# Interleaved multi-query and linear attention on one core: read-outs ahead of flips at a stage's entry, a pause ahead of a weight, and features closed at the second bankful

## The chip, the cores and the metric

The kernel runs on one core of a Trainium2 chip. The metric is the device time of one execution in microseconds (us); the time of the kernel before is the median of three runs. A profile is one further execution, recorded by the hardware. Engines are named as in the profile: PE is TensorE (PEld its weight loads), DVE is VectorE, ACT is ScalarE, POOL is GpSimd, SP is SyncE, whose queue issues nearly all DMAs. L623 is line 623 of the kernel.

## The reference

Four sub-layers are applied to `x` of shape [1, 2048, 576], in float32, each with a layer normalisation without parameters ahead of it and a residual around it:

```python
def _A_ref(x, wq, wk, wv, wo):                 # 32 query heads of 18, one key and value head
    scores = jnp.einsum("bhqd,bkd->bhqk", q, k) * (Dh ** -0.5)
    p = _softmax(scores, axis=-1)
    o = jnp.einsum("bhqk,bkd->bhqd", p, v)
    return ... @ wo

def _B_ref(x, wqkv, w_phi, wo):                # 32 heads of 18, linear attention
    pq = jnp.einsum("bhsd,hdf->bhsf", q, w_phi)
    pk = jnp.einsum("bhsd,hdf->bhsf", k, w_phi)
    phi_q = jnp.concatenate([_softmax(pq), _softmax(-pq)], axis=-1)
    phi_k = jnp.concatenate([_softmax(pk), _softmax(-pk)], axis=-1)
    kv = jnp.einsum("bhsf,bhsd->bhfd", phi_k, v)
    z  = jnp.einsum("bhsf->bhf", phi_k)
    num = jnp.einsum("bhqf,bhfd->bhqd", phi_q, kv)
    den = jnp.einsum("bhqf,bhf->bhq", phi_q, z)[..., None] + 1e-6
    return ... (num / den) @ wo

x = x + _A_ref(_layernorm(x), ...)
x = x + _B_ref(_layernorm(x), ...)
x = x + _A_ref(_layernorm(x), ...)
x = x + _B_ref(_layernorm(x), ...)
```

## The kernel before

Tokens are worked in 16 tiles of 128. The kernel's loop runs over two layers, each an A and a B sub-layer, in two stages.

**The attention stage** goes through score units. For each unit TensorE multiplies keys by queries (`score`, L518), ScalarE takes the exponential (L985), and TensorE multiplies by the values (`values`, L797), which accumulates in a bank of PSUM. Between the bursts of units a generator, `stream`, puts other work, one step a turn: in layer 0 the folding of the feature map into the linear layer's weights (`fold_phi`, L337 to L362), the output projections of finished tiles (`finish_tile`), and for tiles 0 to 12 the linear layer's own keys, values and queries (`mix`). A "bankful" is one half (288 columns) of a projection of one tile. The loads of weights are generators too, advanced once a turn: `load_weight` fetches a weight in five pieces through three staging buffers, and VectorE splits each piece into a high part (L133) and a low part (L134). The order of PE and DVE in this stage is pinned to the order in which the code emits it. One bank of PSUM is free for the other work besides the one that the accumulation leaves, so a matmul of the other work waits until the copy that empties a bank has run.

**Features.** `feature_start` takes a bankful, subtracts the maximum and the minimum of each head and applies the exponential (L551 to L558); `feature_end` sums each head's values and divides (reduce L563, reciprocal L564, multiply L565). With `copies` equal to `V`, as in `mix`, all but the exponential is VectorE's work; with `A`, in the stage's entry, the multiply of L565 is GpSimd's. `update_state` (L595, added at L601) adds a tile's product of features and values to `kv`. The normalised query features of a tile are "flipped" (transposed on TensorE, eleven transposes, L623, and copied by ScalarE, L628) and spilled to DRAM.

**The read-out stage** is entered by `leave()`: the last keys and values, `finish_state` (eight transposes of `kv`, L731, and three DMAs that write the block-diagonal `kvb`, L736), and the queries of three tiles which are left: tile 13 with its features in `featk`, tile 14 in `featq`, tile 15 in `xsc`. Within `leave` the order of PE is pinned. Their flips come behind it, from `flips`. Then `token_tile(i)` runs for all 16 tiles in a pipeline, up to the next stage: it loads the features `pht` (L645), and `read_out` makes 22 matmuls (44 in the profile's count, L748), the division on VectorE (`den`, `xo`, L755 to L758), five transposes (L290, L294), which ScalarE (L131) and VectorE (L134, L299) copy as a high and a low part into `xs`, and the output projection with `wob` (L240, two bankfuls), added to the residual. In layer 0 the next layer's norm and queries follow. Here the tile framework's scheduler orders what is not pinned, and seven banks of PSUM rotate.

Of the kernel before, what the change touches and what calls it, by code (L numbers as in the profile page):

```python
# [61 lines left out]
def kernel(ctx, tc, x_in, wq, wk, wv, wo, wqkv, w_phi, wob, out):  # L62
# [174 lines left out]
    def project(dst, w, c0, xs, after=None, products=range(len(PRODUCTS)), last=LASTP):  # L237
        for j, n in enumerate(products):
            slot, half, k = PRODUCTS[n]
            T.matmul(dst, xs[:, slot, :], w[half][:, k, c0 : c0 + HALF],  # L240
                     start=(n == 0), stop=(n == last))
            if n == last:
                if after is not None:
                    after()
                yield -250
            elif j % 2:
                yield 250
# [4 lines left out]
    def bankful(kind, ps, shape=(P, HALF)):  # L252
        yield Kind(kind)
        return ps.tile(list(shape), F32, name="ps")

    def run(gen):
        for _ in gen:
            pass
# [301 lines left out]
    def feature_end(e, b, E):  # L560
        ev = e[:, b * HH : (b + 1) * HH].rearrange("p h s d -> p (h s) d")
        z = small.tile([P, 2 * HH], F32, name="fz")
        V.tensor_reduce(z, ev, axis=AX.X, op=ALU.add)  # L563
        V.reciprocal(z, z)  # L564
        E.tensor_mul(ev, ev, z[:, :, None].to_broadcast([P, 2 * HH, DH]))  # L565

    def heads(po):
        return po.rearrange("p (h d) -> p h d", d=DH)
# [37 lines left out]
    def queries(xs, e, st, ps, copies):  # L606
        for b in range(2):
            po = yield from bankful("P", ps)
            yield from project(po, st["wpq"], b * HALF, xs, lambda: feature_start(heads(po), e, b, copies))
        if copies is A:  # L610
            for b in range(2):
                feature_end(e, b, G)
        else:
            feature_end(e, 0, V)

    def flip_features(e, pht, ps, copies):
        phi = e.rearrange("p h s d -> p (h s d)")
# [78 lines left out]

    def queries_in(i, xs, eq, st, ps, spill):
        yield from queries(xs, eq, st, ps, A)
        pht = st["sp"].tile([P, NKG, P], F32, name="phs", bufs=2)
        yield from flip_features(eq, pht, ps, A)  # L700
        spill_features(pht, spill, i)
# [169 lines left out]
    def attend(layer, st, a1o, stream):  # L871
# [13 lines left out]
        with ctx1:  # L885
# [11 lines left out]
            def finish_group(c, g):  # L897
                turned = a1.tile([P, CW], F32, name="turned", bufs=2)
                V.transpose(turned, acc[c, g])
                yield STAGE  # L900
                sums = turned.rearrange("p (b f) -> p b f", f=32)
                rd = small.tile([P, CW // 32], F32, name="rd")
                V.reciprocal(rd, sums[:, :, DH])
                V.tensor_mul(sums, sums, rd[:, :, None].to_broadcast([P, CW // 32, 32]))
                yield STAGE
                osb = a1.tile([P, CW], F32, name="osb", bufs=1)
                V.transpose(osb, turned)
                parts = a1.tile([P, 2, CW], F32R, name="parts", bufs=1)
                split(parts[:, 0, :], parts[:, 1, :], osb, V, V)
                keep_group(parts.bitcast(F32), c, g)  # L910
                if g == NG - 1:
                    while c > 0 and c - 1 not in st["added"]:
                        yield STAGE
                    on = heads_in()
                    load_heads(on.bitcast(F32), c)
                    due = at[0] + DUE
                    while at[0] < min(due, len(units)):
                        yield STAGE
                    finished.append((c, on))
                yield STAGE  # L920
# [294 lines left out]
    for layer in range(LAYERS):  # L1215
        last = layer == LAYERS - 1
        st.update(start_state(bw), added=set())
        with tc.tile_pool(name="a1o", bufs=2) as a1o:

            def load(key, place, *args, **kw):  # L1220
                st[key] = weight_tiles(place) if isinstance(place, str) else place.weights()
                yield from reload_weight(key) if key in wd else load_weight(st[key], *args, **kw)

            def load_wo():
                return load("wo", Room(a1o), wo, slice(0, D))

            def load_wv():
                return load("wv", "b", wqkv, slice(2 * D, 3 * D))

            def stream(v, layer=layer):  # L1230
# [34 lines left out]
                loads.append(load_wo())  # L1265
                if layer == 0:
                    yield from wait(lambda: len(loads) > 0)
                    loads.extend((save_weight("wo"), save_weight("wq"), load_wv(), load("wob", "a", wob, slice(0, D)),
                                  save_weight("wob")))

                    def room(name):
                        if name == "wt":
                            return bw.tile([P, 5 * P], F32, name="xn")
                        tag = {"fo": "featk", "bd": "featq"}[name]
                        return bw.tile([P, H, 2, DH], F32, name=tag).rearrange("p h s d -> p (h s d)")

                    for step in fold_phi(ps, room, v.a1):
                        yield step
                        if finished and not isinstance(step, Kind) and (step is STAGE or step < 0):
                            yield from finish_tile()  # L1280
                else:
                    loads.append(load_wv())
# [128 lines left out]
        with psx, tc.tile_pool(name=f"s{layer + 1}", bufs=2) as sp:  # L1411
            if not last:
                reload_w4(sp)

            def leave():
                xn = layer_norm(c, stats, sp, A, "xo")
                advance(second_keys)
                xl = sp.tile([P, 9, P], F32R, name="xs3")
                advance(transposed(xn, xl, ps, A, LOE), 2)
                queued = [queries_in(i, x, feature_room(name), st, ps, spills[layer])  # L1420
                          for i, x, name in ((KEPT, kept, "featk"), (c - 1, xs, "featq"))]
                advance(queued[0])
                both = sp.tile([P, 9, PW], F32R, name="xsc").bitcast(F32).rearrange("p a b -> p (a b)")
                ek, eq = (both[:, k * 2 * D : (k + 1) * 2 * D].rearrange("p (h s d) -> p h s d", s=2, d=DH)
                          for k in range(2))
                last_keys = keys_in(c, xl, ek, st, ps)
                queued.append(queries_in(c, xl, eq, st, ps, spills[layer]))
                advance(last_keys, 2)
                run(load("wob", "a", wob, slice(0, D), engines=(A, V)))
                advance(last_keys, 2)  # L1430
                if not last:
                    run(load("wq", "b", wq, slice(0, D), engines=(A, G)))
                advance(queued[0])
                advance(last_keys)
                advance(queued[2])
                run(finish_state(st, sp, ps))
                advance(queued[2])
                advance(queued[1], 2)
                before = None
                for i in traced(nc)[mark:]:  # L1440
                    if i.engine == mybir.EngineType.PE:
                        if before is not None:
                            tc.add_manual_dep(i, before, NOSYNC, reason="order")
                        before = i.name
                return queued

            def flips(queued):
                for job in queued:
                    run(job)
                    yield STAGE  # L1450

            def room(i):
                if i % 2:
                    return sp.tile([P, NKG, P], F32, name="pht", bufs=1)
                return bw.tile([P, NKG, P], F32, name="pht")

            def token_tile(i):
                pht = room(i)
                load_features(pht, spills[layer], i)
                if i not in left:  # L1460
                    xres[i] = sp.tile([P, D], F32, name="xt", bufs=6)
                    nc.sync.dma_start(xres[i], xd[i])
                yield STAGE
                yield STAGE
                yield from read_out(i, pht, st, sp, ps)
                if last:
                    nc.sync.dma_start(out[i * P : (i + 1) * P, :], xres[i])
                else:
                    nc.sync.dma_start(xd[i], xres[i])
                    yield STAGE  # L1470
                    yield from next_queries(i, None, layer + 1, st, bw, sp, ps)

            order = range(NT)
            st["sp"] = sp
            jobs = [flips(leave()), *[token_tile(i) for i in order]]
            if last:
                run(pipelined(jobs))
            else:
                settle(layer + 1, ps, jobs)

# [26 lines left out]
```

## Time and profile before

| what | us |
|---|---|
| median of three runs | 2711.44 (2710.91 to 2713.7) |
| the profiled execution | 2709.95 |
| its span in the trace | 2708.2 |
| TensorE busy in the span | 2616.8 (97%) |
| ScalarE busy | 2154.5 (80%) |
| VectorE busy | 1236.9 (46%) |

The mean granted clock of TensorE is 0.99 of full speed. The read-out stage of layer 0 begins about 1283 us into the span, that of layer 1 about 2598 us. A row of the timeline gives the start and the length of a group of equal instructions, the engine, the line, the operation, what it writes and reads, and in brackets the idle time of the engine just before it with what ended it. A row such as "PE ps L623 <- POOL featq L565: 8.3, 4, 2.7" in the table of waits says that TensorE's instructions of L623 waited for GpSimd's L565 four times, for 8.3 us together and 2.7 at the longest.

### The profile page before, as it was taken

The numbers are of one execution on the slowest core, as the hardware profiler recorded it, in microseconds if no ns is written. First come the engines' busy times: TensorE is split into PE (matmuls) and PEld (weight loads), VectorE is DVE, ScalarE is ACT, GpSimd is POOL, SyncE is SP. The second block draws the span as 40 slices with busy tenths as digits, with TensorE's granted clock in tenths as the row PEclk, the third lists the DMA queues.
The fourth block names the chain that finished last, engine by engine and source line by source line (L and its number), as shares of the span: only waits on it lengthen the run. The fifth ranks groups of instructions, "written<-read, shape, count | busy, mean of one in ns | idle before, by whom it ended". The sixth has DMA issues, their size and how long they took to land. (4 is left out here: it accounts for less than half of the span.)

```text
span 2708.2 us, 55518 instructions
## 1 busy us (share of the span) xinstructions
PE 2616.8 (97%) x22052; PEld 1447.8 (53%) x22052; DVE 1236.9 (46%) x2839; ACT 2154.5 (80%) x2529; POOL 65.9 (2%) x106
## 2 busy tenths in 40 slices
PE   7989899999999999999999999999999999999999
PEld 6633335554555544437997244444444444444588
DVE  8532244445455444435775124444444444444365
ACT  4578898898989889995334999999999999999721
POOL 1000000000000000001100000000000000000010
PEclk9999999999999999999999999999999999999999
DMA  5564134222223212224645412222222222222164
GB/s 185 160 205 134 52 105 133 72 65 55 59 63 74 62 45 56 58 64 131 197 151 167 146 50 59 59 59 59 59 59 59 59 59 59 56 58 56 39 192 139
DMA packets 469358, 245.06 MB, mean 90 GB/s; under 512 B 213410, under 2 KB 426850, under 8 KB 469090
## 3 DMA queue, kind: packets, MB, share of 16 engines
q1 hardware_dynamic: 467618, 238.46, 31.7%
q8 instruction: 177, 2.90, 0.5%
q10 hardware_dynamic: 1472, 2.95, 0.4%
q14 instruction: 91, 0.75, 0.1%
HBM read 133.86 MB, written 105.51 MB: 88 GB/s over the span
## 5 line engine op out<-in xcount | busy, mean ns | idle before, releaser
L985 ACT ACTIVATE pt<-sc 128x1024 f32<-128x1024 f32 x2036 | 1922.7, 1055 | 206.9 <-PE sc L518 187.2
L518 PE MATMUL sc<-qst,kst 56*128 56x512 f32 x3840 | 699.0, 452 | 26.4 <-ACT pt L985 26.0
L518 PEld LDWEIGHTS sc<-qst,kst 56*128 56x128 f32 x3840 | 320.2, 184 | 566.2 <-ACT pt L985 512.9
L797 PE MATMUL acc<-pt,vst 128*32 128x512 f32 x4096 | 502.6, 602 | 1.5 <-DVE kv L601 0.9
L797 PE MATMUL ps<-pt,vst 128*32 128x512 f32 x4048 | 485.1, 601 | 3.3 <-DVE featk L551 2.9
L797 PEld LDWEIGHTS ps<-pt,vst 128*32 128x32 f32 x4048 | 109.1, 109 | 229.9 <-issue 223.0
L797 PEld LDWEIGHTS acc<-pt,vst 128*32 128x32 f32 x4096 | 104.5, 109 | 213.3 <-issue 207.5
L304 DVE TENSOR_TENSOR xc<-xc,acc 128x288 f32<-128x288 f32 x60 | 27.2, 454 | 339.3 <-PE acc L240 339.3
L240 PE MATMUL ps<-wahi,xs 128*128 128x288 f32 x801 | 173.1, 302 | 2.2 <-ACT xs L131 0.6
L240 PEld LDWEIGHTS ps<-wahi,xs 128*128 128x128 f32 x801 | 130.9, 188 | 10.6 <-issue 2.8
L240 PE MATMUL ps<-walo,xs 128*128 128x288 f32 x445 | 130.3, 295 | 0.0
L240 PE MATMUL acc<-wdhi,on 128*128 128x288 f32 x540 | 119.8, 307 | 1.8 <-DMA on<-od 1.8
L240 PE MATMUL ps<-wchi,xs 128*128 128x288 f32 x504 | 110.9, 305 | 0.0
L396 PE MATMUL ps<-xsc,wbhi 128*128 128x256 f32 x576 | 107.5, 286 | 0.7 <-ACT xsc L131 0.7
L131 ACT ACTIVATE xs<-ps 128x512 fp32r<-128x512 f32 x36 | 21.4, 595 | 105.5 <-PE ps L290 105.4
L418 ACT ACTIVATE pc<-ps 128x256 fp32r<-128x256 f32 x80 | 30.4, 384 | 93.1 <-PE ps L396 92.8
L240 PEld LDWEIGHTS acc<-wdhi,on 128*128 128x128 f32 x540 | 87.9, 187 | 23.5 <-issue 20.6
L551 DVE COPY featq<-ps 128x288 f32<-128x288 f32 x44 | 20.1, 457 | 170.2 <-PE ps L240 170.0
L396 PEld LDWEIGHTS ps<-xsc,wbhi 128*128 128x128 f32 x576 | 91.3, 193 | 1.6 <-ACT xsc L131 1.1
L240 PEld LDWEIGHTS ps<-wchi,xs 128*128 128x128 f32 x504 | 82.2, 188 | 15.7 <-issue 14.5
L271 POOL TENSOR_TENSOR rstd<-var,neghalf 128x1 f32<-128x1 f32 (+1 forms) x56 | 32.0, 571 | 2400.0 <-DVE var L269 2377.9
L240 PE MATMUL acc<-wdlo,on 128*128 128x288 f32 x300 | 88.2, 294 | 0.0
(269 smaller groups left out, 3107.4 us busy)
## 6 DMA issues: line engine op xcount, KB each, us to landing
qst<-qd SPq DMA_DIRECT2D x360, 72.0 KB
od<-parts SPq DMA_DIRECT2D x512, 36.0 KB
pht<-phi SPq DMA_DIRECT2D x32, 540.0 KB
qd<-pc SPq DMA_DIRECT2D x64, 256.0 KB
on<-od SPq DMA_DIRECT2D x60, 256.0 KB
phi<-pht SPq DMA_DIRECT2D x104, 144.0 KB
xd<-xc SPq DMA_DIRECT2D x33, 288.0 KB
flipped<-pht SPq DMA_DIRECT2D x112, 72.0 KB
```

What stands on the lines that cost most here:

```text
L131: A.activation(dst_hi, src, AF.Copy)
L240: T.matmul(dst, xs[:, slot, :], w[half][:, k, c0 : c0 + HALF], start=(n == 0), stop=(n == last))
L271: G.tensor_tensor(rstd, var, neghalf[:, :n], op=ALU.pow)
L304: V.tensor_add(xr, xr, po)
L396: T.matmul(po, lhs, xsc[:, slot, :], start=(n == 0), stop=(n == LASTP))
L418: A.activation(pc[:, 0, :], po, AF.Copy)
L518: T.matmul(sc, kst[head_rows(h), t * P : (t + 1) * P], q[head_rows(h), h // 2, :], start=True, stop=True)
L551: V.tensor_copy(e[:, hs, 0, :], src)
L797: T.matmul(acc[32 * j : 32 * j + 32, :], vst[:, t, :], pts[j], start=first, stop=last)
L985: A.activation(pt, sc, AF.Exp, scale=SCALE)
```

## The change

It has four edits. (1) `queries` closes the features of the first half, when VectorE makes them, as soon as the second bankful has its bank, ahead of the second projection; before, it did so behind both. The two closings of the stage's entry only move into `queries_in`. (2) In the end of a group of attention the second transposition (`osb`) moves from the third turn into the second. (3) In layer 0 five turns pass between the fetch of the value weight and its splits. (4) In the entry of the read-out stage tile 13's flips run inside `leave`, ahead of the second bankful of tile 14's queries; that bankful and the flips of tiles 14 and 15 become late work of the pipeline, which lets one round, three rounds and two rounds pass ahead of them; and tiles 0 and 1 issue their loads ahead of `leave` explicitly.

```diff
     def queries(xs, e, st, ps, copies):
         for b in range(2):
             po = yield from bankful("P", ps)
+            if b and copies is V:
+                feature_end(e, 0, V)
             yield from project(po, st["wpq"], b * HALF, xs, lambda: feature_start(heads(po), e, b, copies))
-        if copies is A:
-            for b in range(2):
-                feature_end(e, b, G)
-        else:
-            feature_end(e, 0, V)
...
     def queries_in(i, xs, eq, st, ps, spill):
         yield from queries(xs, eq, st, ps, A)
+        for b in range(2):
+            feature_end(eq, b, G)
         pht = st["sp"].tile([P, NKG, P], F32, name="phs", bufs=2)
...
                 V.tensor_mul(sums, sums, rd[:, :, None].to_broadcast([P, CW // 32, 32]))
-                yield STAGE
                 osb = a1.tile([P, CW], F32, name="osb", bufs=1)
                 V.transpose(osb, turned)
+                yield STAGE
...
+            def delayed(work, count):
+                yield next(work)
+                for _ in range(count):
+                    yield STAGE
+                yield from work
...
-                    loads.extend((save_weight("wo"), save_weight("wq"), load_wv(), load("wob", "a", wob, slice(0, D)),
+                    loads.extend((save_weight("wo"), save_weight("wq"), delayed(load_wv(), 5), load("wob", "a", wob, slice(0, D)),
...
                 advance(queued[2])
                 run(finish_state(st, sp, ps))
                 advance(queued[2])
-                advance(queued[1], 2)
+                advance(queued[1])
+                run(queued[0])
...
-                return queued
+                return queued[1:]
 
             def flips(queued):
+                for rounds, job, count in ((1, 0, 1), (3, 0, 3), (2, 1, 3)):
+                    for _ in range(rounds):
+                        yield STAGE
+                    advance(queued[job], count)
                 for job in queued:
                     run(job)
-                    yield STAGE
...
-            jobs = [flips(leave()), *[token_tile(i) for i in order]]
+            jobs = [token_tile(i) for i in order]
+            for job in jobs[:2]:
+                next(job)
+            st["late"].append(flips(leave()))
             if last:
-                run(pipelined(jobs))
+                run(pipelined(jobs, st["late"]))
             else:
                 settle(layer + 1, ps, jobs)
```

The order of TensorE's instructions at the entry of the read-out stage of layer 0, before, from the last matmul of tile 14's second bankful on (L623 are the flips of tiles 13, 14 and 15, L748 the read-out of tile 0, L290 and L294 its transposes):

```order
L240 MATMUL ps<-wclo_4384,xs_13975 128x288
L623 MATMUL ps<-idf,featk 108x128 x10
L623 MATMUL ps<-idf,featk 72x128
L623 MATMUL ps<-idf,featq 108x128 x10
L623 MATMUL ps<-idf,featq 72x128
L623 MATMUL ps<-idf,xsc 108x128 x10
L623 MATMUL ps<-idf,xsc 72x128
L748 MATMUL ps<-kvb,pht 64x57 x20
L748 MATMUL ps<-kvb,pht 64x38 x2
L290 MATMUL ps<-idf,xo 128x128 x4
L294 MATMUL ps<-idf,xo 128x128
```

And now, from the last matmul of tile 14's first bankful on:

```order
L240 MATMUL ps<-wclo_4384,xs_13975 128x288
L620 MATMUL ps<-idf,featk 108x128 x10
L620 MATMUL ps<-idf,featk 72x128
L747 MATMUL ps<-kvb,pht 64x57 x20
L747 MATMUL ps<-kvb,pht 64x38 x2
L240 MATMUL ps<-wchi,xs_13975 128x288
...
L290 MATMUL ps<-idf,xo 128x128 x4
L294 MATMUL ps<-idf,xo 128x128
...
L620 MATMUL ps<-idf,featq 108x128 x10
```

Tile 0's read-out and then tile 14's second bankful follow the flips of tile 13; at the second cut stand tile 1's read-out, tile 0's projection, tile 1's transposes and projection and tile 2's read-out. The flips of tile 14 come only then, those of tile 15 behind tile 4's read-out.

VectorE's order in the folding of weights in layer 0, where the value weight (`wbhi`, `wblo`) and then `wob` (`wahi`, `walo`) are split from `wstage`, before:

```order
L357 COPY featk<-ps 128x504
L133 CAST wbhi<-wstage 128x576
L134 TENSOR_TENSOR wblo<-wstage,wbhi 128x576
...
L362 COPY featk<-ps 128x72
L338 COPY xn<-ps 72x128
...
L899 STREAM_TRANSPOSE turned<-acc 128x512
...
L133 CAST parts<-osb 128x512
L134 TENSOR_TENSOR parts<-osb,parts 128x512
L362 COPY featk<-acc 128x72
```

And now:

```order
L357 COPY featk<-ps 128x504
L362 COPY featk<-ps 128x72
L338 COPY xn<-ps 72x128
...
L898 STREAM_TRANSPOSE turned<-acc 128x512
...
L905 STREAM_TRANSPOSE osb<-turned 128x512
L133 CAST wahi<-wstage 128x576
L134 TENSOR_TENSOR walo<-wstage,wahi 128x576
L133 CAST parts<-osb 128x512
L134 TENSOR_TENSOR parts<-osb,parts 128x512
L133 CAST wahi<-wstage 128x576
L134 TENSOR_TENSOR walo<-wstage,wahi 128x576
L362 COPY featk<-acc 128x72
```

Three splits stood between L357 and the first L362, and none does now; around the end of a group, ahead of the second L362, stood none, and two pairs do now.

VectorE's order in `mix`, at the end of a tile's queries, is L551 to L556 of the second half, then L563 to L565 of the first half and L601 before; now L563 to L565 come first, then L551 to L556 and L601. The order of TensorE is the same through all of attention in both layers, and no instruction of an engine is added or removed.

## The prediction

> **What bounds the kernel now.** First the page: the busy shares and the chain that ended last.
>
> ```profile
> span 2708.2 us, 55518 instructions
> PE 2616.8 (97%) x22052; PEld 1447.8 (53%) x22052; DVE 1236.9 (46%) x2839; ACT 2154.5 (80%) x2529; POOL 65.9 (2%) x106
> PE 40%; ACT 3%; issue 1%; DVE 0%; DMA 0%; POOL 0%; ACTq 0%; SPq 0%; DVEq 0%; POOLq 0%
> ```
>
> TensorE is busy 97% of the span. The chain names only part of the span, and nearly all that it names is TensorE's. Next, busy time by stretches: a steady piece of the second attention stage (columns: length, PE, PEld, DVE, ACT, POOL, granted clock, DMA share, GB/s).
>
> ```profile
> 1700.00:1900.00 200.00, 198.13 (x1645) 97.01 (x1648) 91.39 (x183) 184.68 (x201) 1.62 (x3) 1.00 0.25 60
> ```
>
> TensorE has 1.9 us free in 200 at full clock, and the change neither adds nor removes a matmul. So a gain can only come from places where TensorE waits, and a loss only from new waits. The table of waits tells who makes it wait (total, times, longest):
>
> ```profile
> PE ps L623 <- POOL featq L565: 8.3, 4, 2.7
> PE ps L290 <- DVE den L756: 2.0, 2, 1.0
> PE ps L337 <- DVE featk L362: 7.6, 6, 4.5
> ```
>
> The first two rows are the entries of the read-out stages, the third the folding of weights early in layer 0. A few more, on the linear layer's features inside attention, follow below. The parts of the change touch just these.
>
> **Stage entry.** The timeline of TensorE at layer 0's entry, and then at layer 1's (start, length; in brackets the idle time before and what ended it):
>
> ```profile
> 1281.28 0.30 PE L240 MATMUL ps<-wchi,xs 128*128 128x288 f32 x1
> ...
> 1283.14 1.36 PE L623 MATMUL ps<-idf,featk 128*108 128x128 f32 x11
> 1287.17 0.76 PE L623 MATMUL ps<-idf,featq 128*108 128x128 f32 x5 [2.67 <-POOL featq L565]
> 1289.40 1.36 PE L623 MATMUL ps<-idf,featq 128*108 128x128 f32 x6 [1.48 <-POOL featq L565]
> 1290.56 2.62 PE L623 MATMUL ps<-idf,xsc 128*108 128x128 f32 x11
> 1293.10 1.48 PE L748 MATMUL ps<-kvb,pht 108*64 108x57 f32 x44
> 1295.60 0.69 PE L290 MATMUL ps<-idf,xo 128*128 128x128 f32 x4 [1.02 <-DVE den L756]
> ```
>
> ```profile
> 2601.83 0.76 PE L623 MATMUL ps<-idf,featq 128*108 128x128 f32 x5 [2.67 <-POOL featq L565]
> 2604.07 1.53 PE L623 MATMUL ps<-idf,featq 128*108 128x128 f32 x6 [1.48 <-POOL featq L565]
> 2605.39 2.24 PE L623 MATMUL ps<-idf,xsc 128*108 128x128 f32 x11
> 2610.06 0.69 PE L290 MATMUL ps<-idf,xo 128*128 128x128 f32 x4 [1.02 <-DVE den L756]
> ```
>
> Idle time: 2.67 + 1.48 + 1.02 = 5.17 us in each layer. The flips behind it also run slowly: eleven took 1.36 us undisturbed, but the 22 that follow reach from 1287.17 to 1293.10, which less the 1.48 of waiting is 4.45 us in place of 2.72. That is 1.73 us lost, and by the same reckoning (2601.83 to 2605.39 + 2.24) 1.60 in layer 1. The granted clock (seventh column) shows why:
>
> ```profile
> 1291.00:1294.00 3.00, 3.00 (x40) 2.40 (x40) 0.00 (x0) 1.14 (x4) 0.59 (x1) 0.66 0.77 224
> ```
>
> So 6.90 us in layer 0 and 6.77 in layer 1 could go. The change runs tile 13's flips before tile 14's second bankful, then tile 0's read-out, that bankful, tile 0's transposes, tile 1's read-out and the projections; tile 14's flips come after two more read-outs and two projections of two bankfuls each, at least 4 x 1.86 + 2 x 1.48 = 10.4 us behind its own bankful. Its features took 1289.40 - 1283.14 = 6.3 before, so these waits go whole. On SP the loads of the next tiles' features now stand ahead of two tiles' stores instead of behind them, and tile 2 needs its load only after both projections: no price. What counts is what takes the waits' place.
>
> The first new candidate is `kvb`, which the read-out reads. A bankful takes 1283.14 - 1281.28 = 1.86 us, so TensorE now arrives at tile 0 at 1283.14 - 1.86 + 1.36 = 1282.64, ten microseconds earlier than before. The queue of SP:
>
> ```profile
> 1278.44 2.66 SPq L736 DMA_DIRECT2D kvb<-featx  x3
> 1284.57 0.48 SPq L203 DMA_DIRECT2D wblo<-wqd  x1
> 2593.10 2.60 SPq L736 DMA_DIRECT2D kvb<-featx  x3
> ```
>
> The last of the three copies has left at 1281.10. I read from the reuse of its completion lane by the issue at 1284.57 that it had landed by then. The wait is between 0 and 1.93 us, and I take the middle, 1.0. In layer 1 the issue ends at 2595.70 and TensorE arrives some 1.6 us later, but no weight loads stand around it: I take 0.1, with 1.9 as the far end. Tile 0's transposes: before, they started 2.50 us after their read-out did and waited; now 1.48 + 1.86 = 3.34 us lie between, so that wait is covered, with 0.2 for VectorE, which is then still ending tile 14's features. Tile 1's transposes are covered by tile 0's projection. Next in line is the handoff from tile 1's transposes to its own projection, which has lost the read-out that used to lie between. The rows of that handoff before:
>
> ```profile
> 1296.33 0.60 ACT L131 ACTIVATE xs<-ps 128x512 fp32r<-128x512 f32 x1 [1.62 <-PE ps L290]
> 1296.96 0.69 DVE L134 TENSOR_TENSOR xs<-ps,xs 128x512 fp32r<-128x512 f32 x1 [0.82 <-ACT xs L131]
> ```
>
> Uncovered it costs at most 0.60 + 0.69 = 1.29 and at least 0. Four matmuls of the high half and one of a read-out are placed in it, so I take 0.7, and 0.45 (0 to 1.3) for the similar handoffs of the next two tiles. In sum layer 0 pays 1.0 + 0.2 + 0.7 + 0.45 = 2.35 and gains 6.90 - 2.35 = 4.55; layer 1 pays 1.45 and gains 6.77 - 1.45 = 5.3. **Entries: -9.9 us**, with ends of -13.7 (nothing comes back) and about -5 (each price at its far end).
>
> The Trainium skill, "TensorE: Matmul & The Clock Gate", section "HAM oscillation — how this bites in real kernels", says that the clock falls back only after idle gaps above some 3.4 us. By it these short gaps would cost no clock, the 1.73 and 1.60 would stay, and the total gain below would be 3.3 us smaller. The rows above, at 0.66 after gaps of 2.67 and 1.48, contradict it, and so does one below (191.12, eight matmuls in 1.94 in place of 1.06 after a gap of 1.80), so it gets no chance of its own.
>
> **The pause of five turns.** The value weight's splits stand in VectorE's order ahead of a copy that TensorE needs, and wait there for their load:
>
> ```profile
> 164.14 0.46 DVE L133 CAST wbhi<-wstage 128x576 fp32r<-128x576 f32 x1 [5.30 <-DMA wstage<-in_B_wqkv_dram]
> 164.63 0.76 DVE L134 TENSOR_TENSOR wblo<-wstage,wbhi 128x576 fp32r<-128x576 f32 x1
> ```
>
> ```profile
> 158.05 1.06 PE L797 MATMUL acc<-pt,vst 128*32 128x512 f32 x8
> ...
> 167.91 0.43 PE L337 MATMUL ps<-idf,fstage 128*72 128x128 f32 x1 [4.48 <-DVE featk L362]
> 168.27 1.94 PE L797 MATMUL acc<-pt,vst 128*32 128x512 f32 x8
> ...
> 172.76 2.25 PE L797 MATMUL acc<-pt,vst 128*32 128x512 f32 x16
> ...
> 190.76 0.43 PE L337 MATMUL acc<-idf,fstage 128*72 128x128 f32 x1 [1.80 <-DVE featk L362]
> 191.12 1.94 PE L797 MATMUL ps<-pt,vst 128*32 128x512 f32 x8
> ```
>
> The splits now come behind that copy, so the 4.48 falls to the half microsecond that such a round trip may cost: 4.1 gained. The matmuls behind it regain speed: the first eight lost 0.88 (1.94 against 1.06), the sixteen at 172.76 still 0.33 (2.25 against the 1.92 of sixteen at 508.45, below), and the 2.5 us between them, at speeds between those two, some 1.1: 2.3 in all. But two pairs of the next weight's splits (0.46 + 0.76, some 1.2 each) now stand ahead of the same copy one round later, where TensorE already waited 1.80. That wait grows by 2.4, and the slow stretch behind it, as after the longer wait, by some 1.0. Net 4.1 + 2.3 - 2.4 - 1.0: **-3.0 us**, between -6.5 (the later splits run in VectorE's idle time) and +1 (they wait for their load too).
>
> **Query features.** Closing the first half (reduce, reciprocal, multiply) moves ahead of the second half's copy. In one of these tiles (VectorE, then TensorE's waits that follow from it in three of them):
>
> ```profile
> 609.09 0.46 DVE L551 COPY featq<-ps 128x288 f32<-128x288 f32 x1 [4.35 <-PE ps L240]
> ...
> 611.30 0.75 DVE L563 TENSOR_REDUCE fz<-featq 128x32 f32<-128x576 f32 x1
> ...
> 612.47 0.76 DVE L565 TENSOR_TENSOR featq<-featq,fz 128x576 f32<-128x576 f32 x1
> ```
>
> ```profile
> 508.45 1.92 PE L797 MATMUL acc<-pt,vst 128*32 128x512 f32 x16 [0.87 <-DVE kv L601]
> 613.90 0.77 PE L595 MATMUL acc<-featk,vb 128*32 128x36 f32 x64 [1.15 <-DVE turned L899]
> 974.67 4.48 PE L797 MATMUL ps<-pt,vst 128*32 128x512 f32 x24 [2.86 <-DVE featk L551]
> ```
>
> The closing lasts from 611.30 to 613.23, some 1.9 us, and its new place is the 4.35 us in which VectorE waited for TensorE. It delayed the transposition and the `kv` sum that free a bank; 0.87 and 1.15 go. Of the 2.86 I count 0.2, since the work ahead of it starts from the end of an accumulation, not from VectorE. **-2.2 us**, with ends of -4.9 and 0. In layer 1 no such wait exists, so nothing there. The transposition moved by a turn in the group's end changes VectorE's order only beside the weight splits: 0.
>
> **Sum.** 9.9 + 3.0 + 2.2 = 15.1 us off the profiled execution of 2709.95 us (span 2708.2), giving 2694.9. That execution lies 1.5 below the median of the runs, 2711.44, so I predict **2696.4 us**.
>
> **Rivals.** (a) The entry's wait changes its name: TensorE waits for `kvb`, then for each uncovered handoff, the clock stays low, and the entries give a microsecond at most. For it: tile 0 is read ten microseconds sooner, right behind its source's copies. Against: the bound of 1.93. Then 1 + 3 + 2.2 = 6.2 at best, and near 5 with smaller gains elsewhere: about 2706. (b) The pause only shifts the stall: splits meet their loads later, ahead of another copy. For it: the 190.76 row. Worth 0 in place of 3: about 2699.5. (c) Slower: VectorE becomes the bound at the entries. A tile's division chain stands ahead of the next low half in its order:
>
> ```profile
> 1294.30 0.18 DVE L755 TENSOR_SCALAR den<-ps 128x24 f32<-128x24 f32 x1 [5.05 <-PE ps L748]
> 1295.94 0.20 DVE L758 COPY xo<-xo 128x64 f32<-128x64 f32 x1
> ```
>
> It lasts 1296.14 - 1294.30 = 1.84 us. With five tiles in each layer waiting for it, 18.4 us return, against 15.1 gained: 2714.7. It decides above 1.5 us a tile. Against it: the second tile before had the same order and TensorE did not wait there. (d) The scheduler undoes the order, no change at 2711; the engine orders speak against it.
>
> **Numbers.** Forecast 0.64, (a) 0.15, (b) 0.12, (c) 0.06, (d) 0.03. A difference of 0.2% (5.4 us) is about what a measurement tells from none. The low end is everything removed, 13.7 + 6.5 + about 2 = 22 us, 2689; the high end takes in (a), 2707. The forecast's own range is 2691 to 2702. Faster takes the forecast, (b) and half of (a): 0.83; the same takes the rest of (a) and (d): 0.11; slower 0.06.
>
> **What would show it.** Right: at both entries the waits of L620 on POOL are gone, the eleven flips of tiles 14 and 15 take some 1.4 us, and the waits on `kvb` and on the copies of tile 1 stay under 2 us together; near 163 us no 4.48; near 186 us (the 190.76 of before) a wait of about 4 on the same copy; the rows at 508 and 614 without a wait on VectorE. Wrong: a `kvb` wait above 2 us, TensorE waiting for `xs` or `den` in each of the first tiles, or a clock of 0.5 reaching over the first read-outs.

## The result, and the profile after

The changed kernel takes 2695.27 us in the median of four runs (2694.03 to 2697.54), against 2711.18 for the kernel before in the same comparison: a ratio of 0.994, with a 95% interval of 0.9923 to 0.9958. Measured twice more, the ratio is 0.9953 (0.9940 to 0.9967) and 0.9944 (0.9930 to 0.9958). The profiled execution took 2694.40 us. The page:

```profile
span 2692.6 us, 55535 instructions
PE 2609.5 (97%) x22052; PEld 1444.7 (54%) x22052; DVE 1239.0 (46%) x2839; ACT 2153.4 (80%) x2529; POOL 66.2 (2%) x106
PE 40%; ACT 3%; issue 1%; DVE 0%; ACTq 0%; POOL 0%; DVEq 0%; POOLq 0%
```

The shares look as before. TensorE's busy time is 7.3 us shorter with the same number of matmuls: in this profile about half of the gain is matmuls that run faster, and the other half is idle time. In two further profiles of the changed kernel, whose spans are 13.7 and 11.8 us shorter than before, the busy time is shorter by 3.8 and 3.7. The table of waits of the changed kernel (total, times, longest):

```profile
PE sc L518 <- SPq L1007: 6.2, 1, 6.2
PE acc L337 <- DVE featk L362: 4.6, 3, 4.0
PE ps L337 <- DVE featk L362: 3.4, 6, 1.8
PE ps L796 <- DVE featk L551: 2.9, 1, 2.9
PE ps L240 <- ACT xs L131: 1.9, 3, 0.6
PE ps L747 <- DMA kvb<-featx: 1.1, 1, 1.1
PE ps L747 <- DMA pht<-phi: 1.0, 1, 1.0
```

The 8.3 us on GpSimd's L565 are gone, and so are those on L756 and on the `kv` sum; 7.6 on L362 in `ps` has become 3.4, but 2.5 in `acc` has become 4.6 (`ps` and `acc` name the bank that this copy empties). New are `kvb`, `pht` and the second and third wait for L131. TensorE's timeline at layer 0's entry, with rows left out:

```profile
1273.09 1.36 PE L620 MATMUL ps<-idf,featk 128*108 128x128 f32 x11
1275.60 1.48 PE L747 MATMUL ps<-kvb,pht 108*64 108x57 f32 x44 [1.14 <-DMA kvb<-featx]
...
1279.88 0.30 PE L294 MATMUL ps<-idf,xo 128*128 128x128 f32 x1 [0.30 <-DVE xo L757]
...
1286.70 0.40 PE L240 MATMUL ps<-wahi,xs 128*128 128x288 f32 x1 [0.64 <-ACT xs L131]
...
1288.52 0.29 PE L747 MATMUL ps<-kvb,pht 108*64 108x57 f32 x2 [1.03 <-DMA pht<-phi]
...
1293.55 1.41 PE L620 MATMUL ps<-idf,featq 128*108 128x128 f32 x11
```

The flips of tile 14 take 1.41 us without a wait, those of tile 15, at 1304.05, as long, and 3.11 us of waiting stand where 5.17 stood. Layer 1's entry:

```profile
2587.30 1.48 PE L747 MATMUL ps<-kvb,pht 108*64 108x57 f32 x44
...
2591.58 0.30 PE L294 MATMUL ps<-idf,xo 128*128 128x128 f32 x1 [0.30 <-DVE xo L757]
...
2598.40 0.40 PE L240 MATMUL ps<-wahi,xs 128*128 128x288 f32 x1 [0.64 <-ACT xs L131]
...
2604.18 1.41 PE L620 MATMUL ps<-idf,featq 128*108 128x128 f32 x11
```

There only 0.94 us of waiting is left: neither `kvb` nor `pht` is waited for. The folding of weights in layer 0:

```profile
162.82 0.30 PE L337 MATMUL ps<-idf,fstage 128*72 128x128 f32 x1 [0.33 <-DVE featk L362]
...
185.38 0.43 PE L337 MATMUL acc<-idf,fstage 128*72 128x128 f32 x1 [3.97 <-DVE featk L362]
185.74 1.94 PE L796 MATMUL ps<-pt,vst 128*32 128x512 f32 x8
```

The 4.48 fell to 0.33, and the 1.80 at the group's end grew to 3.97, with the slow matmuls (1.94 for eight) behind it.

**Where the time went, by sections.** The same VectorE instruction was looked up in each trace (the transpositions `turned` and the residual additions of L304); the table gives how much earlier or later than before each section ended, with the sections' bounds in times of the kernel before. Negative is faster. The names are those of the experiments below.

| kernel | to 146 | fold, to 224 | to 367 | features, to 967 | entry 0, to 1348 | to 1515 | entry 1, 1605 to 2632 |
|---|---|---|---|---|---|---|---|
| the change | -0.9 | -3.2 | -1.5 | -2.5 | -3.4 | +1.5 | -5.6 |
| the change, again | -0.3 | -4.3 | 0.0 | -2.6 | -2.5 | +1.6 | -5.6 |
| the change, a third time | -0.6 | -3.1 | -0.5 | -2.7 | -1.2 | +1.9 | -5.6 |
| entry_only | -0.1 | +1.6 | -1.4 | -0.1 | -2.2 | +1.5 | -5.6 |
| pause_only | 0.0 | -4.0 | +1.2 | -0.7 | +0.1 | -0.1 | 0.0 |
| close_only | -0.6 | -2.2 | +0.1 | -2.4 | +1.0 | +1.2 | +0.1 |
| osb_only | -0.2 | +1.6 | +1.2 | +0.1 | -0.7 | +0.6 | +0.2 |
| wob_pause | -0.7 | -6.6 | -1.2 | -2.3 | -0.7 | +1.1 | -5.6 |
| wq_late | -0.9 | -3.4 | +1.1 | -2.6 | -4.8 | +0.9 | -5.6 |
| both | -0.2 | -6.5 | +1.3 | -2.5 | -4.8 | +0.9 | -5.6 |
| no_cover | +0.2 | -4.0 | +0.1 | -2.6 | +4.8 | +0.9 | +3.3 |
| read_first | 0.0 | -3.0 | +1.2 | -2.5 | -5.1 | +3.0 | -5.3 |

Between 1515 and 1605 nothing moved. One profile stands for each kernel but the changed one, so a column's scatter is read from the kernels that do not touch it: up to 2 us in the fold, 1.5 behind it, about 1 at entry 0, and 0.2 at entry 1; for the features it is 0.1 in two of three, 0.7 in the third. At entry 0 the three profiles of the changed kernel differ by more, 2.3 us; the part on why the prediction was right says from what.

### The profile page after: what moved, and what is told of

Same layout as the page of the kernel before. It is cut to its first block, busy times and chain, and to the rows that moved or that the text cites. A ratio compares the mean times of both kernels' runs of the same rounds, so it can differ in the third digit from the quotient of the medians.

```text
span 2692.6 us, 55535 instructions
## 1 busy us (share of the span) xinstructions
PE 2609.5 (97%) x22052; PEld 1444.7 (54%) x22052; DVE 1239.0 (46%) x2839; ACT 2153.4 (80%) x2529; POOL 66.2 (2%) x106
## 5 line engine op out<-in xcount | busy, mean ns | idle before, releaser
L304 DVE TENSOR_TENSOR xc<-xc,acc 128x288 f32<-128x288 f32 x60 | 27.2, 454 | 339.5 <-PE acc L240 339.5
L240 PEld LDWEIGHTS ps<-wahi,xs 128*128 128x128 f32 x801 | 130.8, 188 | 12.2 <-issue 3.1
L131 ACT ACTIVATE xs<-ps 128x512 fp32r<-128x512 f32 x36 | 21.4, 595 | 103.7 <-PE ps L290 103.7
L240 PEld LDWEIGHTS ps<-wchi,xs 128*128 128x128 f32 x504 | 82.3, 188 | 15.9 <-issue 14.2
L396 PE MATMUL ps<-xsc,wblo 128*128 128x256 f32 x320 | 85.7, 283 | 0.0
```

What stands on the lines that cost most here:

```text
L131: A.activation(dst_hi, src, AF.Copy)
L304: V.tensor_add(xr, xr, po)
L396: T.matmul(po, lhs, xsc[:, slot, :], start=(n == 0), stop=(n == LASTP))
```

## The experiments

### Each part alone

`entry_only` is the changed kernel with the other three edits undone; the other three put one edit each into the kernel before.

```diff
 # entry_only, against the changed kernel
-            if b and copies is V:
-                feature_end(e, 0, V)
...
+            feature_end(e, 0, V)
...
-                osb = a1.tile([P, CW], F32, name="osb", bufs=1)
-                V.transpose(osb, turned)
                 yield STAGE
+                osb = a1.tile([P, CW], F32, name="osb", bufs=1)
+                V.transpose(osb, turned)
...
-delayed(load_wv(), 5)
+load_wv()
```

```diff
 # pause_only, against the kernel before
-load_wv()
+delayed(load_wv(), 5)
 # close_only, against the kernel before: feature_end(e, 0, V) ahead of the second project in queries
+            if b and copies is V:
+                feature_end(e, 0, V)
...
-            feature_end(e, 0, V)
 # osb_only, against the kernel before
-                yield STAGE
                 osb = a1.tile([P, CW], F32, name="osb", bufs=1)
                 V.transpose(osb, turned)
+                yield STAGE
```

Expected of `entry_only`:

> Only the stage entry is changed. Theory (the terms of the sum are separate and add up): the prediction priced the entries at -9.9 us; the trace of the changed kernel shows 3.2 us less up to the end of layer 0's read-outs, of which 1.4 are lost again in a longer wait for a register load at the head of layer 1's attention, and 5.6 less in layer 1: so -7 to -9 us against before, and the wait at that head 6 us instead of 4.8. Rival (that wait only varies from run to run and has nothing to do with the entry): the wait stays at 4.8 and the gain is -9 or more. Rival (the gain needs the other parts): under -4.

Expected of `pause_only`:

> Only the pause of five turns ahead of the value weight's splits. Theory: the wait of 4.5 near 163 us shrinks to 0.3, the wait at the next group's end grows from 1.8 to about 4, together -3 us, between -2 and -4.5. Rival (the later wait eats all of it): 0 to -1. Rival (the clock recovers everywhere): -5 to -6.5. The wait at the head of layer 1's attention stays at 4.8 if the entry made it longer.

Expected of `close_only`:

> Only the earlier closing of the first half of the query features. Theory: the waits of 0.9 (kv sum) and 1.2 (transposition) in layer 0's attention go, the 2.9 ahead of L551 stays: -2 to -2.6 us. Rival (waits come back elsewhere on the same bank): 0 to -1. Rival (all the waits on VectorE in attention go): -4.9.

Expected of `osb_only`:

> Only the earlier transposition at a group's end. Theory: VectorE's order changes beside two weight splits alone: 0, within 1 us. Rival (the splits there are late then and lengthen the wait of 1.8 near 190 us): +1 to +2.

Measured, against a median of 2709.64 us for the kernel before on the same chip:

| kernel | median us | difference | ratio, 95% interval |
|---|---|---|---|
| entry_only | 2701.49 | -8.2 | 0.9963 (0.9951 to 0.9975) |
| pause_only | 2706.45 | -3.2 | 0.9987 (0.9978 to 0.9997) |
| close_only | 2707.11 | -2.5 | 0.9993 (0.9984 to 1.0002) |
| osb_only | 2710.68 | +1.0 | 1.0 (0.9991 to 1.0009) |

The sizes are those that the theory gave. By the runs alone `close_only` and `osb_only` can't be told from no change, but the column of the features can: -2.3 to -2.7 in all nine profiles of the table that have this edit, -0.7 to +0.1 in the three others that lack it. In the trace of `close_only` the one wait for VectorE of more than half a microsecond that is left among the features is

```profile
PE ps L796 <- DVE featk L551: 2.9, 1, 2.9
```

the one of which the prediction counted almost nothing. So the rival by which all waits go falls.

One idea about `entry_only` fell too. The wait for a register load at the head of layer 1's attention (4.8 us before, 6.2 after) was taken for a place where layer 0's entry gives back 1.4 us. It is 6.6 in `close_only`, whose entry is the old one:

```profile
PE sc L518 <- SPq L1007: 6.6, 1, 6.6
```

Over all profiles it is 4.8, 4.6, 4.3 and 6.6 in the kernels with the old entry, and 5.4 to 6.2 in all with a new one, `no_cover` with its 5.6 among them, which gains nothing at its entries. What sets it was not found; the column "to 1515" of the table is this in most rows, but not in `read_first`, where this wait of 6.0 explains 1.2 of 3.0, and not in `osb_only`.

### Whether the cover by read-outs brings the gain

`no_cover` lets no round pass ahead of the flips; `read_first` puts tile 14's second bankful back into the entry and tile 13's flips into the gap behind tile 0's read-out.

```diff
 # no_cover, against the changed kernel
-((1, 0, 1), (3, 0, 3), (2, 1, 3))
+((0, 0, 1), (0, 0, 3), (0, 1, 3))
 # read_first, against the changed kernel
-                advance(queued[1])
-                run(queued[0])
+                advance(queued[1], 2)
...
-                return queued[1:]
+                return queued
...
-((1, 0, 1), (3, 0, 3), (2, 1, 3))
+((1, 0, 3), (3, 1, 3), (2, 2, 3))
```

Expected of `no_cover`:

> The changed kernel with the rounds ahead of the flips set to none: tile 13's flips still run ahead of tile 14's second bankful, but the flips of tiles 14 and 15 come directly behind that bankful, ahead of all read-outs. Theory (the gain of the entry is the cover of the features' latency by read-outs): the waits on POOL return and the first grows by the 1.36 us of tile 13's flips to 4.0 in each layer, the clock falls again: +9 to +12 against the changed kernel, which is -3 to -7 against before. Rival (the gain comes from tile 13's flips, which now fill the time before the last bankful): 0 to +3 against the changed kernel.

Expected of `read_first`:

> The changed kernel with tile 14's second bankful inside the entry, as before the change, and tile 13's flips in its place behind tile 0's read-out. Theory (it is the cover by read-outs that brings the gain, whichever of the two pieces of work stands in the gap): within 1.5 us of the changed kernel; the wait for kvb is shorter by the 0.5 us that the bankful is longer than the flips, the one for tile 0's xo longer by as much. Rival (tile 13's early flips are the gain): +5 or more.

Expected of the changed kernel, run beside the first and beside the second of them:

> The changed kernel once more, as the measure for the other three. Theory (the parts add up): the parts alone gave -8.2, -3.2 and -2.5 us, so -14 against before, between -12.5 and -16. Rival (they help one another): below -16. Rival (they share a gain): above -12. Its wait for the register load at the head of layer 1's attention is between 4.3 and 6.6 as in all kernels so far, with and without the new entry.

> The changed kernel as a measure beside the two others on the same chip: between -12 and -16 against before.

`no_cover` took 2711.48 us, against 2696.87 for the changed kernel beside it and 2709.05 for the kernel before (ratio 1.0007, 0.9998 to 1.0016): 14.6 us lost, more than the 9 to 12 expected, though the other three edits are still in it. TensorE's timeline at layer 0's entry:

```profile
1281.01 0.76 PE L620 MATMUL ps<-idf,featq 128*108 128x128 f32 x5 [2.71 <-POOL featq L565]
1284.17 1.52 PE L620 MATMUL ps<-idf,featq 128*108 128x128 f32 x6 [2.40 <-POOL featq L565]
1285.49 2.56 PE L620 MATMUL ps<-idf,xsc 128*108 128x128 f32 x11
1287.97 2.34 PE L747 MATMUL ps<-kvb,pht 108*64 108x57 f32 x44
1291.30 0.69 PE L290 MATMUL ps<-idf,xo 128*128 128x128 f32 x4 [0.99 <-DVE den L755]
```

The waits on GpSimd are back, though the first did not grow to 4.0 as expected: 2.71 and 2.40, 5.1 together in place of 4.15. The slow clock now reaches over the first read-out (2.34 us in place of 1.48). New waits come on top: those for `xs` and `xo` are 3.3 us over both entries, 0.6 before. By the table the entries lose 4.8 and 3.3 us against before.

`read_first` took 2693.52 us (2691.24 to 2698.24), the changed kernel beside it 2695.16 (2694.42 to 2698.64): 1.6 us less, where at most 1.5 was expected, and no difference beyond the scatter. Its wait for tile 0's `xo` is 0.71 us, 0.4 longer, as expected; none for `kvb` appears, but none does in the changed kernel's profile beside it either. So what brings the gain is that read-outs lie between tile 14's features and their flips; which of the two pieces of work fills the gap behind tile 0's read-out matters little.

The changed kernel itself gave -12.2 and -15.7 us in these comparisons, and -15.9 at first. The parts alone sum to -13.9 (-12.8 with `osb_only`): they add up, as far as a scatter of some 2 us lets one see.

### The wait at the group's end, and the one for tile 2's features

`wob_pause` puts a second pause ahead of the next weight's splits. `wq_late` moves layer 0's load of `wq` behind three rounds of the read-outs, so that half of it stands behind tile 2's features on SP's queue. `both` has the two edits.

```diff
 # wob_pause, against the changed kernel
-load("wob", "a", wob, slice(0, D)),
+delayed(load("wob", "a", wob, slice(0, D)), 5),
 # wq_late, against the changed kernel: out of leave() ...
-                if not last:
-                    run(load("wq", "b", wq, slice(0, D), engines=(A, G)))
 # ... and into flips()
+                passed = 0
                 for rounds, job, count in ((1, 0, 1), (3, 0, 3), (2, 1, 3)):
                     for _ in range(rounds):
                         yield STAGE
+                        passed += 1
+                        if passed == 3 and not last:
+                            run(load("wq", "b", wq, slice(0, D), engines=(A, G)))
```

Expected of `wob_pause`:

> The changed kernel with a second pause of five turns, between the fetch and the splits of the weight that follows (wob): no split stands ahead of the copy L362 at the group's end. Theory (the two pairs of splits there cost 2.2 us of waiting and keep the clock down): the wait of 4.0 near 185 us falls to 1.8 or less, and the slow stretch behind it shortens: -2 to -3.5 against the changed kernel. Rival (TensorE waits there for the group's own chain, whatever stands beside it): 0 to -0.5. Rival (the splits meet another copy later): 0 to +2, with a new wait on L357 or L362 after 190 us.

Expected of `wq_late`:

> The changed kernel with layer 0's load of wq moved from inside the entry behind three rounds of the read-out's pipeline; half of it now stands behind tile 2's feature load on SP's queue. Theory (TensorE's wait of 1.0 for tile 2's features comes from the weight loads ahead of them): that wait goes, the wait for kvb stays near 1 since two pieces still stand ahead of it: -0.7 to -1.5 against the changed kernel. Rival (the features are late through the reuse of their buffer, or their own time): no change, the wait stays at 1.0 to 1.4. Rival (wq is late for the next layer's queries): +1 to +4 and a wait of L396 or L240 on a load near 1300 us.

Expected of `both`:

> The two that went ahead of the changed kernel together: the second pause ahead of wob's splits, and wq's load behind three rounds. Theory (the two waits lie 1100 us apart and add up): -21 to -22.5 us against before, -8.5 to -10 against the changed kernel; the wait for tile 2's features gone (it was 1.8 with the second pause alone) and the one near 183 us at 1.8. Rival (the gain of wq_late was scatter): as with the second pause alone, -19.

| kernel | median us | before, same chip | difference | ratio, 95% interval |
|---|---|---|---|---|
| wob_pause | 2689.95 | 2709.05 | -19.1 | 0.9929 (0.9915 to 0.9942) |
| wq_late | 2694.36 | 2709.05 | -14.7 | 0.9947 (0.9933 to 0.996) |
| both | 2691.66 | 2710.82 | -19.2 | 0.9929 (0.9915 to 0.9943) |

TensorE in `wob_pause` at the group's end:

```profile
183.47 0.30 PE L337 MATMUL acc<-idf,fstage 128*72 128x128 f32 x1 [1.80 <-DVE featk L362]
183.70 1.24 PE L796 MATMUL ps<-pt,vst 128*32 128x512 f32 x8
```

The wait is 1.80 again: the other 2.2 us of the 3.97 were the two pairs of splits. The fold section gains 6.5 and 6.6 in the two kernels with this pause, against 3.0 to 4.3 in the others with the first pause, so it is worth 2 to 3.5 us, as expected. The medians put `wob_pause` 6.9 us ahead of the changed kernel and `both` 3.5; the first also has the scatter in it.

In `wq_late` and in `both` the wait for tile 2's features does not appear; `wob_pause` alone has 1.8 of it, the changed kernel 1.0 to 1.3. (The wait for `kvb`, expected to stay near 1 in `wq_late`, is 0.2 there.) So the weight loads ahead of it on SP's queue have a part in that wait, and the rivals (the reuse of its buffer, or `wq` coming late) fall. They are not the whole cause. `read_first` has no such wait either, and there all eight loads of `wq` still stand ahead of tile 2's features. What differs is that tile 13's flips come later, so that their store (L637) stands behind that load:

```profile
1281.54 2.27 SPq L643 DMA_DIRECT2D pht<-phi  x1
...
1288.15 0.79 SPq L637 DMA_DIRECT2D phi<-phs  x1
```

In the changed kernel this store stands between the weights and the load and takes 3.0 us of SP's time. The load is late through the weights and the store together, and to take one of them out of its way is enough. Entry 0 gains 4.8 in both kernels with the later `wq` and 5.1 in `read_first`, and 3.4 or less in all profiles with the wait. In the runs this is not seen: the median of `wq_late` lies 2.5 us below the changed kernel, within the scatter, and `both` gave no more than `wob_pause` where 2 to 3 us more were expected, which is the number of the rival by which `wq_late` gained nothing. That the second edit is worth anything is shown by the traces, not by the runs. `wob_pause` and `both` are the fastest of all kernels here.

## Why the prediction was right, point by point

- **The whole.** 2696.4 us was forecast, 2695.27 measured, and 2696.87 and 2695.16 later. On the profile's own scale -15.1 was forecast and -15.6 came, with -13.7 and -11.8 in the other two profiles. That the first came so near is in part luck: layer 0's entry gave 1.1 us less than forecast, and sections that the change hardly touches gave back 0.9 in sum (-0.9 to 146, -1.5 to 367, +1.5 to 1515).
- **Layer 1's entry.** -5.3 forecast, -5.6 in every kernel that has the new entry, save `read_first` (-5.3) and `no_cover`. The removed 5.17 of waiting and 1.60 of slow matmuls, less 0.94 of waits (0.30 for `xo`, 0.64 for `xs`), is 5.8. The price of 0.1 for `kvb` was right: it is not waited for.
- **Layer 0's entry.** -4.55 forecast, -0.7 to -3.4 in the five profiles that have this entry and the wait for tile 2's features. Counted from 1212 us on, behind a fall of the clock near 967 us that lasts longer in two of them, it is -1.7 to -3.3. The prices of `kvb` (1.0 forecast, 1.14, and 0.3 or nothing in the other profiles of it), of tile 0's transposes (0.2, and 0.30) and of the bare handoff of tile 1 (0.7, and 0.64) fit. What failed is a step that was dismissed: of tile 2's feature load the prediction said "tile 2 needs its load only after both projections: no price". It cost 1.0 to 1.8 us of waiting. One reason is that the load leaves SP late; here it is in SP's queue, behind the weights and the store of tile 13's flips:

```profile
1277.18 0.57 SPq L637 DMA_DIRECT2D phi<-phs  x1
1277.86 2.31 SPq L638 DMA_DIRECT2D phi<-phs  x1
1280.26 0.42 SPq L642 DMA_DIRECT2D pht<-phi  x1
1280.73 4.17 SPq L643 DMA_DIRECT2D pht<-phi  x1
```

  The second piece alone, 36 KB, held SP for 4.17 us until 1284.90, and TensorE could read only at 1288.52. The other reason is that TensorE comes to it early: the scheduler puts one matmul of tile 2's read-out (1288.52, x2 in the profile's count) behind the first four of tile 1's projection, and the other 21 only behind the rest, at 1292.14. The prediction had counted that one matmul ("one of a read-out") among those in tile 1's handoff, but not asked what it reads.

  This wait also costs clock. Here are the wait and the stretch behind it in the changed kernel's second profile (the granted clock is the third number from the end), and then the same stretch in the first:

```profile
1288.76 0.29 PE L747 MATMUL ps<-kvb,pht 108*64 108x57 f32 x2 [1.08 <-DMA pht<-phi]
```

```profile
1290.00:1292.00 2.00, 2.00 (x10) 2.00 (x10) 1.11 (x1) 0.44 (x1) 1.51 (x2) 0.50 0.42 126
```

```profile
1290.00:1292.00 2.00, 2.00 (x17) 1.98 (x15) 1.71 (x3) 0.64 (x1) 1.32 (x2) 1.00 0.29 87
```

  The clock fell behind the wait in four of the five profiles; only in the first, after a wait of 1.03, did it not. In `wq_late`, `both` and `read_first`, which lack the wait, it stays at 1.00 through this entry. In the second profile it is 0.59, 0.50, 0.50 and 0.70 in the four microseconds from 1289 on, which makes some 1.7 us lost (an estimate from these four figures): all of the 1.73 that the prediction had gained there. The 0.45 forecast for later handoffs is not seen as a wait of its own; the read-outs that the scheduler spread over the projections cover them. From 1212 us on each of the five profiles gained 0.2 to 0.8 us less than 6.90 less its waits and, where the clock fell, 1.7; what takes this stays open.
- **The clock.** That the short waits at the entry cost clock was right: the flips of tiles 14 and 15 run in 1.41 us each without them, and `no_cover` shows the slow clock again. That all of it comes back was right in layer 1, where the clock stays at 1.00 in every kernel with the cover, and in layer 0 only in the profiles named above. The 3.4 us of the Trainium skill's "TensorE: Matmul & The Clock Gate", section "HAM oscillation — how this bites in real kernels", which the prediction weighed, would have left these microseconds in place.
- **The pause.** -3.0 forecast: the section moved by -3.0 to -4.3 and the runs of `pause_only` by -3.2. All four terms are in the trace: 4.48 to 0.33; 1.80 to 3.97, where 1.80 + 2.4 was forecast; full speed behind the first, and half speed for longer behind the second.
- **The features.** -2.2 forecast, -2.5 to -2.7 in the three profiles. The 0.87 and 1.15 went, and the 2.86 stayed at 2.85, as was argued from the chain ahead of it. The moved transposition: 0 forecast, +1.0 in the runs with an interval on both sides of zero.
- **The rivals.** (a) was right for a part of layer 0 only. (b) was half right, and was in the sum: the pause does shift a stall, and `wob_pause` shows that the shifted part was worth 2 us of waiting. (c) did not happen: past tile 1 no tile waits for `den` or `xo` at these entries.

## What to carry to other kernels

An engine's stage entry that waits for a chain on other engines is mended by work that is ready, and the price is read from what that work itself needs: list each of its inputs with the time at which its load leaves the queue, the later tiles' too, since all are now wanted sooner, and look up in the engine's order the first matmul that reads it, not the bulk of them. What stands ahead of such a load in the queue counts, stores as well as loads. Where a pause moves work out of the way of one copy, look up in the engine's order which copy it stands ahead of next; here half of the pause's gain was paid back one round later, and a second pause fetched it. Where a matmul engine's clock falls after short waits, price a removed wait with the slow matmuls behind it (here these were a third as much again at the entry), and a new wait too.

## What the runs showed of the hardware

The clock fell after waits that are short. In `wob_pause`, right behind a wait of 1.80 us (columns as in the table of stretches before):

```profile
185.00:187.00 2.00, 2.00 (x9) 1.25 (x10) 0.00 (x0) 1.23 (x2) 0.00 (x0) 0.50 0.47 125
```

And it differs between executions where the work does not. The same stretch in the kernel before, and then in the changed kernel, busy to the same 3.05 us of 4 in the first of the two rows:

```profile
244.00:248.00 4.00, 3.05 (x21) 1.08 (x17) 0.23 (x2) 4.00 (x5) 0.00 (x0) 1.00 0.00 0
248.00:252.00 4.00, 4.00 (x22) 1.22 (x20) 0.28 (x1) 1.40 (x3) 0.00 (x0) 0.57 0.21 78
```

```profile
240.00:244.00 4.00, 3.05 (x21) 1.13 (x17) 0.36 (x2) 4.00 (x6) 0.00 (x0) 1.00 0.00 0
244.00:248.00 4.00, 4.00 (x32) 1.09 (x24) 0.16 (x1) 2.81 (x4) 0.00 (x0) 1.00 0.21 78
```

Four microseconds at 0.57 in the one, at full clock in the other, for the same instructions. The Trainium skill, "TensorE: Matmul & The Clock Gate", Part 1, says that the window by which the clock is set runs free, so that the same kernel meets it differently from run to run; these rows agree. Such a fall costs some 1.4 us (the section "to 367": -1.5 to +1.3 in kernels that are nearly alike there). The runs of one kernel differ by more, by 3.5 us among the first four of the changed kernel and by 8.9 among the 28 of the kernel before beside `entry_only`. The clock goes with it: of these 28, the eight at a mean granted clock of 0.990 or 0.991 took 2708.3 us on average, the twelve at 0.988 2710.8, and the two at 0.987 2715.8. That falls like this one make up the whole difference was not shown. A difference of 1 to 2 us between two single profiles says nothing here; the section in which it lies says more.
